# A gated recurrence followed by a maxout layer: folded weights, another opening order, and chunks turned block by block

## The chip, the core and the metric

The kernel runs on one core of a Trainium2 chip. The metric is the device time of one execution in microseconds (us), the median of several runs. Names used below: PE is TensorE (matrix products and transposes), PEld its weight loads, DVE is VectorE, ACT is ScalarE, POOL is GpSimd, SP is SyncE, whose queue issues most of the transfers.

## The reference

Two stages, one after the other. The first is a gated recurrence over the sequence, per batch and channel; the second takes the larger of two linear maps of its output and projects it back.

```python
# x, f_logit: (4, 6144, 256)   lower_bound: (256,)
sig = 1 / (1 + exp(-f_logit))
f = lower_bound + (1 - lower_bound) * sig
i = 1 - f
for t in range(S):
    h = f[:, t] * h + i[:, t] * x[:, t]
    y[:, t] = h
# y as 24576 rows of 256;  w1, w2: (256, 1024)   w_out: (1024, 256)
out = maximum(y @ w1, y @ w2) @ w_out
```

## The kernel before

The rows are cut into 48 blocks of 512. Two rewritings shape the kernel. With om = 1 - lower_bound and u = sigmoid(-f_logit), the input gate is i = om * u, so the factor om is taken out of the recurrence and folded into the weights. And maximum(h1, h2) = h1 + relu(h2 - h1), so the hidden layer is one product with om * (w2 - w1), followed by a relu; what belongs to h1 is a linear map w1 @ w_out, worked out once (w13). The products with the hidden layer (H), the relus (R) and the projections (P, L) are the bulk of the work.

The first four blocks (NP = 4) are loaded in fp32 and transposed on TensorE. All later blocks come in chunks of two (CB = 2): GpSimd issues a cast of the chunk to bf16 in DRAM, and the SP queue issues a transposing transfer from there into SBUF.

```python
def cast(c):                      # chunk c: 2 blocks of f_logit, then of x, into DRAM in bf16
    for name, src in (("fs", f_logit), ("xs", x)):
        nc.gpsimd.dma_start(out=spare[c % NS, name][:], in_=src[b, k * TB : (k + CB) * TB, :], ...)

def turn_dma(c):                  # one transposing transfer for f, one for x; ttpool has 3 buffers of each
    for s, name in enumerate(("fs", "xs")):
        t = ttpool.tile([P, KC, CB * TB], BF16, name=("fT", "xT")[s])
        turned[c, s] = t
        nc.sync.dma_start_transpose(out=t[:], in_=spare[c % NS, name][:])

def cast_behind(c):               # a copy of one column of fT: the next casts wait for its landing
    if c + 1 < NCH:
        last = CB * TB - 1
        nc.gpsimd.tensor_copy(out=held[:], in_=turned[c, 0][:, KC - 1, last : last + 1])
        cast(c + 1)
```

The weights are loaded in quarters of 256 columns (w11 is quarter 1 of w1, wo0 the first quarter of w_out's rows) and prepared on the chip:

```python
def diff(k, h, eng):              # D: wdf = w2 - w1, fp32, 128 x 256
    eng.tensor_tensor(out=wdf[:, h, cols], in0=w2n[:, h, cols], in1=w1n[:, h, cols], op=ALU.subtract)

def scale(k, h, on_dve):          # SC: wd = om * wdf, bf16
    o, i, m = wd[:, h, cols], wdf[:, h, cols], om[:, h : h + 1]
    if on_dve:
        nc.vector.tensor_scalar_mul(out=o, in0=i, scalar1=m)
    else:
        nc.scalar.activation(out=o, in_=i, func=AF.Copy, scale=m)
```

The order of the opening is given by two lists. Every engine works through its own instructions in the order of the list. A letter after the point names the engine (a ScalarE, v VectorE, p GpSimd).

```python
LOADS = """
f0a x0a f0b x0b w11 w21 w13 w23 w12 w22 wo1 w10 f1a w20 wo3 x1a f1b wo2 x1b wo0
f2b f2a x2a x2b f3 x3
"""
PLAN = """
G0a keeps_T TU0a keeps RW1.p F0a0.a V0a F0a1.v warm2 TV0a S0a0 G0b warm5 TU0b
...
"""
```

The items: G the sigmoid, V the product of u and x, TU and TV their transposes on TensorE, F the forget factor, S the scan (the recurrence itself), RW and RO the rounding of w1 and w_out to bf16, TW and KW the transposes of w1 and their copy out of PSUM, W the products for w13 and KL their copy, H hidden products (a and b are the halves of a block), R relus, P and L projections, O the copy of an output, warm products on zeros that keep TensorE busy, CA the start of the first chunk. W130 is W for quarter 0: it needs wo0.

Five PSUM buffers (ps_d) serve the hidden products and all transposes, three (ps_o) the outputs. After the opening comes a regular loop: for each block and each of 8 column groups, one hidden product with its relu and one part of the projection of the block before, with gate, drive, forget and scan of a later block placed at fixed points.

Of the kernel before, what the change touches and what calls it, by code (L numbers as in the profile page):

```python
# [9 lines left out]
BF16 = mybir.dt.bfloat16  # L10
ALU = mybir.AluOpType
# [5 lines left out]
def kernel(  # L17
# [36 lines left out]
    scratch = ctx.enter_context(  # L54
        tc.tile_pool(name="scratch", bufs=1, space=bass.MemoryType.DRAM)
    )
    ttpool = ctx.enter_context(tc.tile_pool(name="turned", bufs=3))
    midpool = ctx.enter_context(tc.tile_pool(name="mid", bufs=2))
    ypool = ctx.enter_context(tc.tile_pool(name="ypool", bufs=4))
    rpool = ctx.enter_context(tc.tile_pool(name="rpool", bufs=3 * FC))  # L60
# [113 lines left out]
            )  # L174

    def turn_dma(c):
        for s, name in enumerate(("fs", "xs")):
            t = ttpool.tile([P, KC, CB * TB], BF16, name=("fT", "xT")[s])
            turned[c, s] = t
            nc.sync.dma_start_transpose(out=t[:], in_=spare[c % NS, name][:])  # L180

    def cast_behind(c):

        if c + 1 < NCH:
            last = CB * TB - 1
            nc.gpsimd.tensor_copy(out=held[:], in_=turned[c, 0][:, KC - 1, last : last + 1])  # L186
            cast(c + 1)

    def part(j, s):
        c, o = divmod(j - NP, CB)  # L190
        return turned[c, s][:, :, o * TB : (o + 1) * TB]

    def gate(j):
        ffs[j] = midpool.tile([P, KC, TB], BF16, name="ff")
        ys[j] = ypool.tile([P, KC, TB], BF16, name="y")
        us[j] = midpool.tile([P, KC, TB], BF16, name="u")
        nc.scalar.activation(out=us[j][:], in_=part(j, 0), func=AF.Sigmoid, scale=-1.0)  # L197

    def drive(j):
        vs[j] = midpool.tile([P, KC, TB], BF16, name="v")  # L200
        nc.vector.tensor_tensor(out=vs[j][:], in0=us[j][:], in1=part(j, 1), op=ALU.mult)  # L201

    def forget_half(j, h, on_act=False):
        forget(ffs[j][:, h, :], us[j][:, h, :], h, on_act)
# [107 lines left out]
    def copy_out(j, g, on_act=False):  # L312
# [3 lines left out]
        else:  # L316
            nc.vector.tensor_copy(out=osbs[j, g][:], in_=pos[j, g, 0][:])  # L317

    def send_out(j, g):
        r0 = j * TB + 2 * g * P  # L320
        nc.sync.dma_start(
            out=out[r0 : r0 + 2 * P, :].rearrange("(p r) d -> p r d", r=2),
            in_=osbs[j, g][:],
        )

    def store(j, g):
        copy_out(j, g)
# [47 lines left out]
        )  # L375
        nc.vector.tensor_scalar_add(out=nom[:], in0=pt, scalar1=-1.0)

    def diff(k, h, eng):
        cols = slice(k * QF, (k + 1) * QF)
        eng.tensor_tensor(  # L380
            out=wdf[:, h, cols], in0=w2n[:, h, cols], in1=w1n[:, h, cols], op=ALU.subtract
        )

    def scale(k, h, on_dve):
        cols = slice(k * QF, (k + 1) * QF)
        o, i, m = wd[:, h, cols], wdf[:, h, cols], om[:, h : h + 1]
        if on_dve:
            nc.vector.tensor_scalar_mul(out=o, in0=i, scalar1=m)  # L388
        else:
            nc.scalar.activation(out=o, in_=i, func=AF.Copy, scale=m)  # L390

    def turn_w1(k):
        pts[k] = ps_d.tile([P, 2, D], BF16, name="dT")
# [49 lines left out]


    LOADS = """
    f0a x0a f0b x0b w11 w21 w13 w23 w12 w22 wo1 w10 f1a w20 wo3 x1a f1b wo2 x1b wo0
    f2b f2a x2a x2b f3 x3
    """
    PLAN = """
    G0a keeps_T TU0a keeps RW1.p F0a0.a V0a F0a1.v warm2 TV0a S0a0 G0b warm5 TU0b  # L450
    F0b0.a S0a1 D10.p RW3.p V0b warm5 TW1 D11.v F0b1.a SC11.a SC10.a TV0b D30.p S0b0
    S0b1 warm6 H02a H03a RW2.p D31.v SC31.v D21.v KW1.a TW3 H02b H03b SC30.a D20.p
    RW0.p RO1.v R02.a TW2 KW3.v SC21.a H06a H06b H07b R03.a H07a W131 SC20.v R06.v
    P020 H04a TW0 P031 H04b D01.p KW2.v P021 G1a KW0.v RO3.v D00.p R07.a R04.a V1a
    P030 TU1a H05a SC01.a H05b SC00.a G1b R05.a F1a1.v P060 F1a0.v P070 P071 P061
    W133 TV1a H00b RO2.p S1a1 V1b H01b TU1b H00a H01a F1b0.a W132 P050 P041 TV1b
    S1a0 P051 R01.a P040 R00.a RO0.a CA H10a H12a F1b1.v H11a G2b H16a P001 S1b0
    W130 G2a P000 S1b1 P010 H10b H16b KL1.v R10.v H11b KL0.a H12b P011 R12.a L00
    R11.a TU2a H14b V2b TU2b V2a H14a H17a R16.a H17b O00.a R14.a G3b L01 R17.a TV2a
    L11 F2a1.v L10 F2b1.v F2a0.v P160 F2b0.v TV2b P100 P120 TU3b P121 S2a0 H13b G3a  # L460
    F3b0.a O01.a S2b0 P140 S2a1 S2b1 H15b P101 H13a P161 P171 R13.a H15a F3b1.v TU3a
    R15.a H24 R24.a H22 V3a H26 F3a1.v F3a0.v R22.a V3b P111 TV3a P170 P141 H20 TV3b
    H23 R26.a P110 H21 S3a1 S3a0 S3b1 P130 P150 S3b0 R20.a H25 R23.a H27 R27.v R21.a
    P151 P131 O10.a R25.a O11.v
    """

    engines = {"a": nc.scalar, "v": nc.vector, "p": nc.gpsimd}
# [18 lines left out]
    def issue(item):  # L486
        name, _, e = item.partition(".")
        eng, on_dve, on_act = engines.get(e), e == "v", e == "a"
        kind = name.rstrip("0123456789ab")
        arg = ["ab".index(c) if c in "ab" else int(c) for c in name[len(kind) :]]  # L490
        if kind == "warm":
            keep_warm(arg[0])
        elif name == "keeps_T":
            turn_bound()
        elif name == "keeps":
            keeps()
        elif kind in ("G", "V") and len(arg) == 2:
            (gate_nat if kind == "G" else drive_nat)(arg[0], 2 * arg[1], 2 * arg[1] + 2)
        elif kind in ("TU", "TV"):
            turn_pe(arg[0], "UV".index(kind[1]), arg[1])  # L500
        elif kind == "F" and len(arg) == 3:
            j, x, h = arg
            tok = slice(x * HB, (x + 1) * HB)
            forget(ffs[j][:, h, tok], uT[j, x][:, h, :], h, on_act)
        elif kind == "S" and len(arg) == 3:
            j, x, h = arg
            scan(j, h, x * HB, (x + 1) * HB, vT[j, x][:, h, :])
        elif kind == "RW":
            round_w1(arg[0], eng)
        elif kind == "RO":  # L510
            round_wout(arg[0], eng)
        elif kind == "D":
            diff(arg[0], arg[1], eng)
        elif kind == "SC":
            scale(arg[0], arg[1], on_dve)
        elif kind == "TW":
            turn_w1(arg[0])
        elif kind == "KW":
            keep_w1(arg[0], eng)
        elif kind == "W":  # L520
            linear_weights(int(name[3]))
        elif kind == "KL":
            keep_linear(arg[0], on_dve)
        elif kind == "H":
            (hidden_half if len(arg) == 3 else hidden_whole)(*arg)
        elif kind == "R":
            relu(arg[0], arg[1], on_dve)
        elif kind == "P":
            pair_steps(arg[0], arg[2], [arg[1]])
        elif kind == "L":  # L530
            pair_steps(arg[0], arg[1], [FC, FC + 1])
        elif kind == "O":
            copy_out(arg[0], arg[1], on_act)
            outs.append(arg)
            send_pending()
        elif kind == "CA":
            nc.gpsimd.tensor_copy(out=held[:], in_=ins[2][1][:, 1, D - 1 : D])
            cast(0)
            turn_dma(0)
            cast_behind(0)  # L540
            send_pending()
        else:
            raise ValueError(item)
# [7 lines left out]
    with tc.manual_schedule():  # L551
        for j in range(NP):
            alloc_in(j)
        nc.scalar.dma_start(out=lbr[:], in_=lower_bound.rearrange("(h p) -> h p", p=P))
        for name in LOADS.split():
            load_item(name)
        nc.vector.memset(warm[:], 0.0)  # L557
        make_identity(nc, ident[:])
        nc.vector.tensor_copy(out=ident_b[:], in_=ident[:])
        keep_warm(7)  # L560
        for item in PLAN.split():
            issue(item)
        assert not outs

        for j in range(3, NBLK + 1):
            for fc in range(FC):
                if j < NBLK:
                    hidden(j, fc)
                project(j - 1, fc)
                if fc == 0 and j > 3:  # L570
                    store(j - 2, 1)
                if fc == 4 and j < NBLK:
                    store(j - 1, 0)
                if j == NBLK and fc in (3, 5, 7):
                    if fc == 3:
                        store(j - 1, 0)
                    else:
                        store_row(j - 1, 1, (fc - 5) // 2)
                if (j, fc) in gate_of:
                    b = gate_of[j, fc]  # L580
                    gate(b)
                    drive(b)
                    for h in range(KC):
                        forget_half(b, h, b == NP)
                        scan_half(b, h)
                if (j, fc) in turn_of:
                    turn_dma(turn_of[j, fc])
                    cast_behind(turn_of[j, fc])
# [30 lines left out]
```

## Time and profile before

| | |
|---|---|
| time, median of 3 runs | 397.82 us (397.27 to 398.25) |
| span of the profiled execution | 395.7 us |
| granted TensorE clock | 1.0 |
| PE busy | 390.5 us |
| ACT busy | 274.4 us |
| DVE busy | 251.3 us |
| POOL busy | 36.7 us |
| bytes moved by DMA | 79.12 MB |

Busy time is summed over the whole span. The products are pipelined and their ends are modelled, so a fully busy PE says only that it had no gap. A group line gives the source line of the kernel, the engine, the operation, what is written and read, and the count; in the timeline the first two columns are the start and the duration in us, and a bracket at the end gives the idle time of the engine just before and what ended it.

### The profile page before, as it was taken

The page shows a single profiled execution, that of the slowest core. Times are in us where ns is not written, and L with a number is a line of the kernel's source. Part 1 is how long each engine was busy: PE and PEld are TensorE (multiplying, and loading weights), DVE is VectorE, ACT ScalarE, POOL GpSimd, SP SyncE. Part 2 cuts the span into 40 slices and gives each one's busy share as a digit, 9 for nine tenths or more (in the row PEclk, how much of TensorE's full clock was granted, in tenths as well). Part 3 has the DMA queues.
Part 4 walks back from the last instruction along what each step waited for, and adds up shares of the span by engine and source line. Part 5 has one row for each costly group of instructions (what it writes and reads, how often), then busy time and mean ns, then how long its engine had stood idle before and what let it go on. Part 6 is the DMA issues. An engine that isn't in the chain of part 4 may idle for free.

```text
span 395.7 us, 7192 instructions
## 1 busy us (share of the span) xinstructions
PE 390.5 (99%) x2842; PEld 275.2 (70%) x2842; DVE 251.3 (63%) x365; ACT 274.4 (69%) x453; POOL 36.7 (9%) x82
## 2 busy tenths in 40 slices
PE   8999999999999999999999999999999999999996
PEld 4796777776666777776667777767677777676775
DVE  4886865756755775576567656755775576567622
ACT  3787876677667666766676677667766766676661
POOL 2511011001201101101101011011011010000000
PEclk9999999999999999999999999999999999999999
DMA  7999999999999999999889899999998999991122
GB/s 227 352 258 206 217 223 195 239 199 208 259 199 200 212 202 221 236 209 216 206 195 210 162 227 183 235 209 195 200 207 208 188 194 225 193 188 55 53 81 107
DMA packets 125078, 79.12 MB, mean 200 GB/s; under 512 B 94194, under 2 KB 101620, under 8 KB 125044
## 3 DMA queue, kind: packets, MB, share of 16 engines
q1 hardware_dynamic: 113072, 55.59, 57.5%
q0 software_dynamic: 11968, 23.07, 35.5%
q8 instruction: 22, 0.36, 0.4%
q14 instruction: 12, 0.10, 0.1%
q10 hardware_dynamic: 4, 0.00, 0.0%
HBM read 53.48 MB, written 48.23 MB: 257 GB/s over the span
## 4 chain that ended last, share of the span: by engine, by line
PE 96%; DMA 1%; DVE 1%; SPq 1%; issue 0%; DVEq 0%
PE psO L268 53%; PE dT L245 40%; PE dT L225 1%; DMA w2n<-in_moe_w_dram 1%; PE dT L126 1%; DVE wdf L380 0%; SPq L100 0%; PE psO L413 0%; DVE y L149 0%; SPq L344 0%; DVE row L332 0%; DVE w1T L355 0%; DVE wob L355 0%; DVE wd L388 0%; PE dT L396 0%
## 5 line engine op out<-in xcount | busy, mean ns | idle before, releaser
L240 ACT ACTIVATE rt<-dT 128x512 bf16<-128x512 f32 x381 | 222.6, 596 | 104.1 <-PE dT L245 102.3
L268 PE MATMUL psO<-wob,rt 128*128 128x256 bf16 x1536 | 230.4, 273 | 0.0
L245 PE MATMUL dT<-y,wd 128*128 128x512 bf16 x736 | 218.4, 379 | 0.0
L268 PEld LDWEIGHTS <-rt 128*128 128x128 bf16 x1536 | 150.1, 98 | 94.9
L149 DVE TENSOR_TENSOR_SCAN y<-ff,y,v 128x512 bf16<-128x512 bf16 x82 | 105.2, 1283 | 2.9
L317 DVE COPY osb<-psO 128x512 f32<-128x512 f32 x92 | 62.1, 679 | 66.9 <-PE psO L268 66.9
L245 PEld LDWEIGHTS <-wd 128*128 128x128 bf16 x736 | 71.9, 98 | 8.9
L268 PE MATMUL psO<-w,y 128*128 128x256 bf16 x384 | 72.4, 273 | 0.0
L201 DVE TENSOR_TENSOR v<-u,xT 128x1024 bf16<-128x1024 bf16 x44 | 30.4, 692 | 61.2 <-ACT u L197 52.2
L197 ACT ACTIVATE u<-fT 128x1024 bf16<-128x1024 bf16 x44 | 46.1, 1048 | 1.2 <-DMA fT<-fs 1.1
L268 PEld LDWEIGHTS <-y 128*128 128x128 bf16 x384 | 37.5, 98 | 4.3
L186 POOL CAST held<-fT 128x1 f32<-128x1 bf16 x21 | 4.7, 226 | 279.4 <-DMA fT<-fs 279.4
L138 DVE TENSOR_SCALAR ff<-u,nom 128x512 bf16<-128x512 bf16 x86 | 29.1, 339 | 0.0
L170 POOL DMA_DIRECT2D fs<-in_f_logit_dram x22 | 12.3, 558 | 5.2 <-issue 5.0
L170 POOL DMA_DIRECT2D xs<-in_x_dram x22 | 12.1, 549 | 0.3 <-issue 0.3
L149 DVE TENSOR_TENSOR_SCAN y<-nff,y,dT 128x256 bf16<-128x256 bf16 x14 | 9.8, 735 | 2.2 <-PE dT L126 2.1
L225 PE MATMUL dT<-y,wd 128*128 128x256 bf16 x64 | 9.8, 273 | 1.0 <-DVE w1T L355 0.8
L433 PE MATMUL psO<-warm 128*128 128x512 bf16 x25 | 8.5, 484 | 1.2 <-DVE warm L557 1.2
L149 DVE TENSOR_TENSOR_SCAN y<-ff,v 128x512 bf16<-128x512 bf16 x6 | 7.4, 1225 | 0.2
L225 PEld LDWEIGHTS <-wd 128*128 128x128 bf16 x64 | 5.9, 98 | 2.2 <-issue 1.0
L108 ACT ACTIVATE un<-fn 128x512 bf16<-128x512 f32 x8 | 5.1, 637 | 1.9 <-DMA fn<-in_f_logit_dram 1.5
L433 PEld LDWEIGHTS <-warm 128*128 128x128 bf16 x25 | 2.7, 120 | 4.0 <-issue 1.8
(42 smaller groups left out, 58.2 us busy)
## 6 DMA issues: line engine op xcount, KB each, us to landing
out_dram<-osb SPq DMA_DIRECT2D x95, 256.0 KB, 3.2
fs<-in_f_logit_dram POOLq DMA_DIRECT2D x22, 512.0 KB, 6.6
xs<-in_x_dram POOLq DMA_DIRECT2D x22, 512.0 KB, 9.5
fn<-in_f_logit_dram SPq DMA_DIRECT2D x6, 256.0 KB, 6.0
xn<-in_x_dram SPq DMA_DIRECT2D x6, 256.0 KB, 5.3
w1n<-in_moe_w_dram SPq DMA_DIRECT2D x4, 256.0 KB, 6.0
w2n<-in_moe_w_dram SPq DMA_DIRECT2D x4, 256.0 KB, 6.0
won<-in_moe_w_out_dram SPq DMA_DIRECT2D x4, 256.0 KB, 6.2
```

Of the source, the lines that this page charges most:

```text
L108: nc.scalar.activation(out=us[j][:, q0:q1, :], in_=ins[j][0][:, q0:q1, :], func=AF.Sigmoid, scale=-1.0)
L138: nc.vector.tensor_scalar(out=o, in0=i, scalar1=nom[:, h : h + 1], scalar2=1.0, op0=ALU.mult, op1=ALU.add)
L149: nc.vector.tensor_tensor_scan(out=ys[j][:, h, t0:t1], data0=ffs[j][:, h, t0:t1], data1=v, initial=initial, op0=ALU.mult, op1=ALU.add,)
L170: nc.gpsimd.dma_start(out=spare[c % NS, name][:], in_=src[b, k * TB : (k + CB) * TB, :], max_dma_last_dim=4096,)
L197: nc.scalar.activation(out=us[j][:], in_=part(j, 0), func=AF.Sigmoid, scale=-1.0)
L201: nc.vector.tensor_tensor(out=vs[j][:], in0=us[j][:], in1=part(j, 1), op=ALU.mult)
L225: nc.tensor.matmul(dts[j, fc][:, tok], lhsT=wd[:, kc, unit(fc)], rhs=ys[j][:, kc, tok], start=(first and kc == 0), stop=(not first and kc ...
L240: nc.scalar.activation(out=rt[:], in_=dts[j, fc][:], func=AF.Relu)
L245: nc.tensor.matmul(dts[j, fc][:], lhsT=wd[:, kc, unit(fc)], rhs=ys[j][:, kc, :], start=(kc == 0), stop=(kc == KC - 1),)
L268: nc.tensor.matmul(ps, lhsT=lhsT, rhs=rhs, start=start, stop=stop, skip_group_check=True)
L317: nc.vector.tensor_copy(out=osbs[j, g][:], in_=pos[j, g, 0][:])
L433: nc.tensor.matmul(idle[:].rearrange("p r d -> p (r d)"), lhsT=warm[:, 0:P], rhs=warm[:], start=True, stop=True,)
```

## The change

It has five parts.

1. The weights are folded as om * w2 - om * w1. The first product (item A) needs w1 alone and may run on any engine; the second (item B) is one fused multiply and subtract on VectorE. It is meant to shorten what follows the landing of w2.
2. The order of the loads and of the opening's list is new; three quarters of w1 are loaded ahead of w2. The item CA stands at the end of the list, and the first casts wait for the landing of f's second half of block 2 (before: of x's first half).
3. A chunk is turned block by block: four transposes (f and x of the first block, then of the second) into six smaller buffers of each kind.
4. The copy that holds the next casts back reads the x of the chunk's first block instead of the f of the whole chunk. It is meant to bound what the casts collide with.
5. In the loop the forget factors are worked out ahead of the drive product, and the stores of blocks 45 and 46 are split in two.

```diff
-    ttpool = ctx.enter_context(tc.tile_pool(name="turned", bufs=3))
+    ttpool = ctx.enter_context(tc.tile_pool(name="turned", bufs=6))
...
     def turn_dma(c):
-        for s, name in enumerate(("fs", "xs")):
-            t = ttpool.tile([P, KC, CB * TB], BF16, name=("fT", "xT")[s])
-            turned[c, s] = t
-            nc.sync.dma_start_transpose(out=t[:], in_=spare[c % NS, name][:])
+        b0, n = NP + c * CB, CB
+        for o in range(n):
+            for s, name in enumerate(("fs", "xs")):
+                t = ttpool.tile([P, KC, TB], BF16, name=("fT", "xT")[s])
+                turned[b0 + o, s] = t
+                nc.sync.dma_start_transpose(
+                    out=t[:], in_=spare[c % NS, name][o * TB : (o + 1) * TB, :]
+                )

     def cast_behind(c):
         if c + 1 < NCH:
-            last = CB * TB - 1
-            nc.gpsimd.tensor_copy(out=held[:], in_=turned[c, 0][:, KC - 1, last : last + 1])
+            b0, n = NP + c * CB, CB
+            nc.gpsimd.tensor_copy(out=held[:], in_=turned[b0, n - 1][:, KC - 1, TB - 1 : TB])
             cast(c + 1)
...
     def send_out(j, g):
+        if NBLK - 4 < j < NBLK - 1:
+            for r in range(2):
+                nc.sync.dma_start(out=rows_out(j, g)[:, r, :], in_=osbs[j, g][:, r, :])
+        else:
+            nc.sync.dma_start(out=rows_out(j, g), in_=osbs[j, g][:])
...
-    def diff(k, h, eng):
+    def fold_w1(k, h, eng):
         cols = slice(k * QF, (k + 1) * QF)
-        eng.tensor_tensor(
-            out=wdf[:, h, cols], in0=w2n[:, h, cols], in1=w1n[:, h, cols], op=ALU.subtract
-        )
-
-    def scale(k, h, on_dve):
+        o, i, m = wdf[:, h, cols], w1n[:, h, cols], om[:, h : h + 1]
+        if eng is nc.scalar:
+            nc.scalar.activation(out=o, in_=i, func=AF.Copy, scale=m)
+        else:
+            eng.tensor_scalar_mul(out=o, in0=i, scalar1=m)
+
+    def fold_diff(k, h):
         cols = slice(k * QF, (k + 1) * QF)
...
+        nc.vector.scalar_tensor_tensor(
+            out=wd[:, h, cols],
+            in0=w2n[:, h, cols],
+            scalar=om[:, h : h + 1],
+            in1=wdf[:, h, cols],
+            op0=ALU.mult,
+            op1=ALU.subtract,
+        )
...
     LOADS = """
-    f0a x0a f0b x0b w11 w21 w13 w23 w12 w22 wo1 w10 f1a w20 wo3 x1a f1b wo2 x1b wo0
-    f2b f2a x2a x2b f3 x3
+    f0a x0a f0b x0b w12 w11 w13 w21 wo1 w23 w22 wo3 f1a w10 w20 x1a f1b wo2 x1b wo0
+    f2a x2a f2b x2b f3 x3
     """
     PLAN = """
-    G0a keeps_T TU0a keeps RW1.p F0a0.a V0a F0a1.v warm2 TV0a S0a0 G0b warm5 TU0b
-    F0b0.a S0a1 D10.p RW3.p V0b warm5 TW1 D11.v F0b1.a SC11.a SC10.a TV0b D30.p S0b0
-    S0b1 warm6 H02a H03a RW2.p D31.v SC31.v D21.v KW1.a TW3 H02b H03b SC30.a D20.p
-    RW0.p RO1.v R02.a TW2 KW3.v SC21.a H06a H06b H07b R03.a H07a W131 SC20.v R06.v
-    P020 H04a TW0 P031 H04b D01.p KW2.v P021 G1a KW0.v RO3.v D00.p R07.a R04.a V1a
-    P030 TU1a H05a SC01.a H05b SC00.a G1b R05.a F1a1.v P060 F1a0.v P070 P071 P061
-    W133 TV1a H00b RO2.p S1a1 V1b H01b TU1b H00a H01a F1b0.a W132 P050 P041 TV1b
-    S1a0 P051 R01.a P040 R00.a RO0.a CA H10a H12a F1b1.v H11a G2b H16a P001 S1b0
-    W130 G2a P000 S1b1 P010 H10b H16b KL1.v R10.v H11b KL0.a H12b P011 R12.a L00
...
+    G0a V0a keeps_T TU0a warm1 TV0a keeps A20.p F0a1.a S0a1 G0b RW1.p F0a0.a warm7
+    TU0b V0b F0b0.a S0a0 A11.p warm2 TV0b F0b1.a RW2.a A31.p A10.a S0b0 S0b1 B10 B11
+    warm4 TW2 TW1 RW3.a KW1.a warm2 TW3 RO1.a A21.v A30.p warm3 H03a H02a H03b B31
+    B30 KW2.a KW3.v B21 B20 H02b RO3.p W131 H06a R02.a H06b A00.p R06.v R03.a RW0.v
+    H07a P020 P021 H07b G1a W133 H05a H05b R07.a P061 A01.p H04a R05.a H04b B00 TW0
+    TU1a RO2.p B01 V1a P070 P030 H00a R04.a F1a1.v H01b H01a KW0.a TV1a P031 P060
+    F1a0.v G1b H00b TU1b S1a1 P071 R01.a V1b S1a0 P051 P050 W132 R00.a P040 F1b0.a
+    TV1b P041 H10a H14a F1b1.a H16a H13a S1b0 RO0.a G2a S1b1 W130 V2a P001 KL0.a
+    P010 H13b H10b P000 R13.v H16b TU2a F2a1.v H14b KL1.a L00 R10.a G2b R14.v P011
+    R16.a V2b L01 TU2b TV2a P161 F2a0.a O00.a H17b F2b0.v L11 H12a G3a H17a H15b
...
     """
...
         elif kind == "CA":
-            nc.gpsimd.tensor_copy(out=held[:], in_=ins[2][1][:, 1, D - 1 : D])
+            nc.gpsimd.tensor_copy(out=held[:], in_=ins[2][0][:, 3, D - 1 : D])
...
                     gate(b)
+                    for h in range(KC):
+                        forget_half(b, h, b == NP)
                     drive(b)
                     for h in range(KC):
-                        forget_half(b, h, b == NP)
                         scan_half(b, h)
```

More of the change, by code (lines that the diff above doesn't have):

```diff
@@ L176, in turn_dma @@
     def turn_dma(c):
-        for s, name in enumerate(("fs", "xs")):
-            t = ttpool.tile([P, KC, CB * TB], BF16, name=("fT", "xT")[s])
-            turned[c, s] = t
-            nc.sync.dma_start_transpose(out=t[:], in_=spare[c % NS, name][:])
+        b0, n = NP + c * CB, CB
[6 more added lines that the diff above has]
+                )
     def cast_behind(c):
         if c + 1 < NCH:
-            last = CB * TB - 1
-            nc.gpsimd.tensor_copy(out=held[:], in_=turned[c, 0][:, KC - 1, last : last + 1])
+            b0, n = NP + c * CB, CB
+            nc.gpsimd.tensor_copy(out=held[:], in_=turned[b0, n - 1][:, KC - 1, TB - 1 : TB])
             cast(c + 1)
-    def part(j, s):
-        c, o = divmod(j - NP, CB)
-        return turned[c, s][:, :, o * TB : (o + 1) * TB]
     def gate(j):
@@ L196, in gate @@
         us[j] = midpool.tile([P, KC, TB], BF16, name="u")
-        nc.scalar.activation(out=us[j][:], in_=part(j, 0), func=AF.Sigmoid, scale=-1.0)
+        nc.scalar.activation(out=us[j][:], in_=turned[j, 0][:], func=AF.Sigmoid, scale=-1.0)
     def drive(j):
         vs[j] = midpool.tile([P, KC, TB], BF16, name="v")
-        nc.vector.tensor_tensor(out=vs[j][:], in0=us[j][:], in1=part(j, 1), op=ALU.mult)
+        nc.vector.tensor_tensor(out=vs[j][:], in0=us[j][:], in1=turned[j, 1][:], op=ALU.mult)
     def forget_half(j, h, on_act=False):
@@ L317, in copy_out, with rows_out @@
             nc.vector.tensor_copy(out=osbs[j, g][:], in_=pos[j, g, 0][:])
+    def rows_out(j, g):
+        r0 = j * TB + 2 * g * P
+        return out[r0 : r0 + 2 * P, :].rearrange("(p r) d -> p r d", r=2)
     def send_out(j, g):
[L320 to L323, printed above, removed]
-        )
+        if NBLK - 4 < j < NBLK - 1:
[3 more added lines that the diff above has]
+            nc.sync.dma_start(out=rows_out(j, g), in_=osbs[j, g][:])
     def store(j, g):
@@ L376, in keeps @@
         nc.vector.tensor_scalar_add(out=nom[:], in0=pt, scalar1=-1.0)
-    def diff(k, h, eng):
+    def fold_w1(k, h, eng):
         cols = slice(k * QF, (k + 1) * QF)
-        eng.tensor_tensor(
-            out=wdf[:, h, cols], in0=w2n[:, h, cols], in1=w1n[:, h, cols], op=ALU.subtract
-        )
-    def scale(k, h, on_dve):
[L385 to L390, printed above, removed]
+        o, i, m = wdf[:, h, cols], w1n[:, h, cols], om[:, h : h + 1]
[4 more added lines that the diff above has]
+    def fold_diff(k, h):
+        cols = slice(k * QF, (k + 1) * QF)
+        nc.vector.scalar_tensor_tensor(
[5 more added lines that the diff above has]
+            op1=ALU.subtract,
+        )
     def turn_w1(k):
@@ L453 @@
-    RW0.p RO1.v R02.a TW2 KW3.v SC21.a H06a H06b H07b R03.a H07a W131 SC20.v R06.v
-    P020 H04a TW0 P031 H04b D01.p KW2.v P021 G1a KW0.v RO3.v D00.p R07.a R04.a V1a
-    P030 TU1a H05a SC01.a H05b SC00.a G1b R05.a F1a1.v P060 F1a0.v P070 P071 P061
-    W133 TV1a H00b RO2.p S1a1 V1b H01b TU1b H00a H01a F1b0.a W132 P050 P041 TV1b
-    S1a0 P051 R01.a P040 R00.a RO0.a CA H10a H12a F1b1.v H11a G2b H16a P001 S1b0
-    W130 G2a P000 S1b1 P010 H10b H16b KL1.v R10.v H11b KL0.a H12b P011 R12.a L00
-    R11.a TU2a H14b V2b TU2b V2a H14a H17a R16.a H17b O00.a R14.a G3b L01 R17.a TV2a
@@ L460 @@
[L460 to L464, printed above, removed]
+    G0a V0a keeps_T TU0a warm1 TV0a keeps A20.p F0a1.a S0a1 G0b RW1.p F0a0.a warm7
+    TU0b V0b F0b0.a S0a0 A11.p warm2 TV0b F0b1.a RW2.a A31.p A10.a S0b0 S0b1 B10 B11
@@ new lines @@
+    P010 H13b H10b P000 R13.v H16b TU2a F2a1.v H14b KL1.a L00 R10.a G2b R14.v P011
+    R16.a V2b L01 TU2b TV2a P161 F2a0.a O00.a H17b F2b0.v L11 H12a G3a H17a H15b
+    R17.a F2b1.v S2a1 H15a S2a0 P101 H12b TV2b S2b1 R15.a R12.a P140 P100 S2b0 TU3a
+    P170 G3b F3a0.v H11a O01.a F3a1.v L10 H11b P141 H20 R11.a P131 H27 R27.a H22 V3a
+    H25 R20.v V3b P121 TV3a R22.a S3a1 TU3b P171 R25.a S3a0 P160 H21 TV3b P110
+    F3b0.a P150 H24 P120 F3b1.a H23 P151 R21.a R24.a S3b0 P111 S3b1 H26 P130 R26.v
@@ L465 @@
+    R23.a O11.a O10.v CA
     """
@@ L511, in issue @@
             round_wout(arg[0], eng)
[L512 to L515, printed above, removed]
+        elif kind == "A":
+            fold_w1(arg[0], arg[1], eng)
+        elif kind == "B":
+            fold_diff(*arg)
         elif kind == "TW":
```

## The prediction

> **What bounds the kernel now.** I read the page first: busy times, slices, and the chain that ended last.
>
> ```profile
> PE 390.5 (99%) x2842; PEld 275.2 (70%) x2842; DVE 251.3 (63%) x365; ACT 274.4 (69%) x453; POOL 36.7 (9%) x82
> ...
> PE   8999999999999999999999999999999999999996
> ...
> DMA  7999999999999999999889899999998999991122
> ...
> PE 96%; DMA 1%; DVE 1%; SPq 1%; issue 0%; DVEq 0%
> ```
>
> TensorE carries 96% of the chain and is full from the second slice to the last; the other compute engines are below 70%. The DMA engines look full too, so they are the first rival. A busy TensorE may still be doing nothing useful, because the opening runs products on zeros. So next I cut the span into stages (columns: stretch, its length, then busy time and instructions of PE, PEld, DVE, ACT, POOL, the granted clock, the DMA share and GB/s).
>
> ```profile
> 13.70:392.40 378.70, 378.70 (x2776) 269.33 (x2775) 242.55 (x347) 267.50 (x441) 31.25 (x70) 1.00 0.94 198
> 0.00:13.70 13.70, 11.55 (x66) 5.92 (x67) 8.29 (x18) 6.92 (x13) 5.45 (x13) 1.00 0.82 263
> ```
>
> From 13.70 us TensorE never stops. No product is removed by the change, so it can win only the part of the first 13.70 us that isn't useful work, or lose by a new hole later. The timeline of TensorE shows that opening.
>
> ```profile
> 9.31 1.46 PE L433 MATMUL psO<-warm 128*128 128x512 bf16 x6
> 10.88 0.61 PE L225 MATMUL dT<-y,wd 128*128 128x256 bf16 x4
> 11.33 0.39 PE L396 MATMUL dT<-ident_b,w1b 128*128 128x128 bf16 x4
> 11.55 0.60 PE L225 MATMUL dT<-y,wd 128*128 128x256 bf16 x4
> 12.02 0.40 PE L396 MATMUL dT<-ident_b,w1b 128*128 128x128 bf16 x4
> 12.26 0.60 PE L225 MATMUL dT<-y,wd 128*128 128x256 bf16 x4
> 13.70 0.60 PE L225 MATMUL dT<-y,wd 128*128 128x256 bf16 x4 [0.84 <-DVE w1T L355]
> ```
>
> The first real products start at 10.88; the next hole ends at 13.70, released by VectorE's copy of w1T, which frees a PSUM buffer. VectorE's own timeline says why that copy was late.
>
> ```profile
> 8.90 0.99 DVE L380 TENSOR_TENSOR wdf<-w2n,w1n 128x256 f32<-128x256 f32 x1 [0.64 <-DMA w2n<-in_moe_w_dram]
> ...
> 11.10 0.40 DVE L380 TENSOR_TENSOR wdf<-w2n,w1n 128x256 f32<-128x256 f32 x1
> ...
> 12.03 0.94 DVE L380 TENSOR_TENSOR wdf<-w2n,w1n 128x256 f32<-128x256 f32 x1
> 12.90 0.41 DVE L355 CAST wob<-won 128x512 bf16<-128x512 f32 x1
> 13.24 0.41 DVE L355 COPY w1T<-dT 128x512 bf16<-128x512 bf16 x1
> ```
>
> The same subtraction takes 0.40 or 0.94 to 0.99 us. The long ones began while GpSimd ran one of its own (8.88 to 9.60 and 11.93 to 12.70).
>
> **What the Trainium skill says.** "SBUF — State Buffer", section "Who interferes with whom": a VectorE instruction with two SBUF inputs competes with a GpSimd instruction that reads SBUF; the later one waits for the whole of the other. The three subtractions agree: 0.40 against 0.94 and 0.99. The new fused operation also has two SBUF inputs, so it can be held in the same way. "VectorE: DVE Perf Modes", section on the fixed extra latency of SBUF sources: an fp32 two-tensor operation takes (N+151)/0.96 ns, that is 424 ns at N=256; the trace has 396. I take 0.40 us for the fused operation too: an estimate, since no row here holds one. "DMA: Bandwidth & Descriptors", "Specifications", gives some 358 GB/s from HBM to a core; here the loads move 351 GB/s between 9 and 24 us. So the loads arrive at a fixed pace, and their order is what can be chosen.
>
> **The change part by part.** I use one unit: a group of two 256-wide products, or of four 128-wide transposes. Between 13.70 and the product W130 (which needs the last quarter to arrive of w_out, wo0) at 22.02 stand 38 such units by the plan: 8.32/38 = 0.219 us each. Before 13.70, 13 units were done (4 input transposes, 3 of w1, 6 of hidden products), so 13.70 - 13 x 0.219 = 10.85 us of TensorE were lost.
>
> *Landings.* By issue and time to landing, the loads in places 5 to 20 land at 8.1, 8.8, 9.5, 10.3 (between its neighbours), 11.0, 11.8, 12.6, 13.3, 14.1, 14.8, 15.6, 16.3, 17.1, 17.8, 18.6 and 20.8. The new order puts w1's quarters 2, 1, 3 in places 5 to 7, w2's quarter 1 in 8, wo1 in 9, w2's 3 and 2 in 10 and 11, wo3 in 12.
>
> *Fold.* Before: subtract (0.40 to 0.99), then a scaling after it (ScalarE 0.51, VectorE 0.55 to 0.58), both after w2. Now om*w1 needs w1 alone and only one operation of 0.40 follows w2. First hidden products: w2's quarter 1 lands at 10.3 instead of 8.8 (1.5 later), the two fused operations run to about 11.1, or 11.6 if GpSimd's A30 and A31 hold them. They start at 11.1 to 11.6 instead of 10.88, so the first product is later by 0.2 to 0.7. Quarter 3: 11.8, two operations, 12.7; quarter 2: after the w1T copy (0.41), 13.8. TensorE from 11.4: four units to 12.3, W131 to 12.7, then H06a straight away, and six units later quarter 2 is there. So it is full from about 12.8, with 13 units done: 12.8 - 13 x 0.219 = 9.95 us lost, against 10.85. **First sum: -0.9 us.**
>
> *What takes it back.* ScalarE rounds the last w_out quarter as soon as it lands.
>
> ```profile
> 20.88 0.62 ACT L355 CAST wob<-won 128x512 bf16<-128x512 f32 x1 [0.20 <-DMA won<-in_moe_w_out_dram]
> ...
> 22.02 0.60 PE L413 MATMUL psO<-wob,w1T 128*128 128x256 bf16 x4
> ```
>
> wo0 is in place 20 in both orders. In the new plan 50 units precede W130 (51 before). Undisturbed it would be reached at 9.95 + 50 x 0.219 = 20.9; but the rounded quarter can't be there before 20.83 + 0.05 + 0.62 + 0.06, about 21.56. TensorE would wait 0.66. Then 21.56 - 50 x 0.219 = 10.61 is lost, against 10.85. **Second sum: -0.24 us.** If wo0 keeps the 0.75 spacing of its predecessors (it came 2.2 after the one in front), nothing is taken back.
>
> *Transposes block by block.* Two chunk transposes become four half ones; bytes and issue time (2.69 and 2.27 us median) stay about the same. The next casts now wait for the first block's f and x, instead of for the whole f. Those waits hardly reach anyone now:
>
> ```profile
> ACT u L197 <- DMA fT<-fs: 1.1, 1, 1.1
> ...
> DVE v L201 <- DMA xT<-xs: 1.5, 1, 1.5
> ```
>
> In steady state a chunk takes TensorE 2 x 7.82 = 15.6 us, and the early gates fall 13.0 to 15.9 us apart. Waiting for x costs up to 3 us of casting once. An estimate of the new chain: casts 10, the transpose of x about 4, gate 0.5: 14.5, still under 15.6. I put 0 here.
>
> *Forget before drive, split stores.* VectorE waits for u either way (52.2 us, off the path): 0. The split stores are of blocks 45 and 46, after the bulk of the DMA: 0 to 0.1 at the tail, whose row copy and last store aren't changed.
>
> **Rivals.** (1) *The opening gains in full*, because wo0 lands at about 19.4: -0.9, 396.9. For it: the 2.2 us step looks like an accident of one transfer. Against it: total bytes and queue are the same. (2) *The DMA becomes the bound*, four small transposes and a later gate costing more than a chunk's slack: each us over 15.6 comes back up to 20 times, 400 to 415. For it: the DMA row of nines. Against it: 14.5 against 15.6, and the slack of several us visible in one short wait out of 44. (3) *New holes in blocks 1 to 3*: V2a stands ahead of R13, R14 and the block 2 work on VectorE and waits for x2a (about 22.3), with five PSUM buffers in turn: +0.3 to +1.0, so 397.9 to 398.6. For it: that one queue stop. Against it: ScalarE serves R10 and R16 beside it.
>
> **Range and chances.** The second sum gives 397.6, the first 396.9; the third rival pulls up. I take 397.4, and 396.4 to 398.5, which also covers the spread of the time before (397.27 to 398.25). Two per cent are 8 us: the opening hasn't that much to give, since more than 5 us of its loss is waiting for the first bytes. Faster by over 2%: 0.01. Slower: 0.02, all of it rival 2.
>
> **What would show it.** Right: first hidden products at 11.1 to 11.6, TensorE full from about 12.8, then one wait on ScalarE's wob before W130 near 21.5; fused operations of 0.4 us, or about 0.9 beside GpSimd; 15.6 us per chunk after. Rival 1: W130 before 21.2 without a wait. Rival 2: TensorE waiting for scans, VectorE for xT, after 60 us. Rival 3: TensorE gaps between 22 and 35 us. I am wrong if the full stage starts after 13.5, or if more than 0.5 us of TensorE gaps stand after 23.

## The result and the profile after

The changed kernel is slower than the one before: ratio 1.010, 95% interval 1.0057 to 1.0142, some 4 us. Its four executions took 400.84, 402.52, 407.19 and 409.70 us, where those of the kernel before stay within 397.27 to 398.25. The ratios here leave out executions over 1.5% longer than the same kernel's fastest, of this kernel the last two, so its loss may be understated. The profiled execution is the fastest; its span is 399.1 us, 3.4 more than before. The page, by the same lines as were read before:

```profile
PE 390.4 (98%) x2796; PEld 274.7 (69%) x2843; DVE 247.4 (62%) x363; ACT 274.3 (69%) x456; POOL 40.7 (10%) x81
...
DMA  7999998999999999999999999999998999989523
...
PE 84%; DMA 10%; ACT 3%; issue 1%; SPq 1%; POOL 1%; DVE 0%; ACTq 0%
```

The busy times hardly moved, and the row of TensorE is the same. The row of the DMA engines ends in 9523 instead of 1122: the transfers no longer finish ahead of the products. The chain moved most: transfers now hold 10% of it instead of 1%, 7% of it the transposes of f. A row of tenths is too coarse for small holes, so the stages have to be asked for (columns: stretch, length, busy time and count of PE, PEld, DVE, ACT, POOL, clock, DMA share, GB/s):

```profile
300.00:350.00 50.00, 48.54 (x337) 33.06 (x342) 29.61 (x42) 32.45 (x54) 5.00 (x9) 1.00 1.00 193
350.00:380.00 30.00, 29.48 (x207) 20.35 (x210) 19.09 (x28) 21.04 (x35) 1.67 (x3) 1.00 0.80 194
```

In the kernel before, TensorE was full here (its line from 13.70 to 392.40 in the prediction). Some matmul records are missing, so a second clock is wanted: VectorE's copy of each finished output. Up to 298 us it starts at nearly the same time in both kernels (79.42 and 79.55, 298.38 and 298.51); at the end it is at 390.49 and 393.83. So the opening cost 0.13 us, and the other 3.2 us came after 298 us, in steps. The chain that ended last names them (start, duration, what):

```profile
296.18 5.28 DMA fT<-fs
301.57 1.06 ACT u L197
302.62 1.47 ACT rt L240 x3
...
312.77 5.37 DMA fT<-fs
318.25 1.06 ACT u L197
...
329.73 5.08 DMA fT<-fs
```

Each time a transpose of f comes too late: ScalarE, which works in order, stands before its sigmoid, the relus behind it are late, and TensorE waits for those. The totals of the waits for these transfers (total us, times, longest) were 1.1 and 1.5 before:

```profile
ACT u L197 <- DMA fT<-fs: 15.0, 10, 2.8
DVE v L201 <- DMA xT<-xs: 10.6, 10, 3.3
```

The steps are 16.6 and 17.0 us apart, one per chunk, and a chunk costs TensorE 15.64 (two blocks of 7.82). They come late because the kernel starts with blocks in hand: up to 182 us no sigmoid waits for its f. The first that does waits 0.84 us, and the wait has grown to 2.77 at 318.25; the first small waits don't reach TensorE.

```profile
190.90 1.06 ACT L197 ACTIVATE u<-fT 128x1024 bf16<-128x1024 bf16 x1 [0.84 <-DMA fT<-fs]
```

So the transfers use up the lead and then set the pace. GpSimd's copy that lets the next casts go marks each turn:

```profile
304.11 0.64 POOL L190 CAST held<-xT 128x1 f32<-128x1 bf16 x1 [15.18 <-DMA xT<-xs]
304.68 0.55 POOL L170 DMA_DIRECT2D fs<-in_f_logit_dram  x1
...
321.28 0.64 POOL L190 CAST held<-xT 128x1 f32<-128x1 bf16 x1 [15.51 <-DMA xT<-xs]
321.86 0.55 POOL L170 DMA_DIRECT2D fs<-in_f_logit_dram  x1
```

The SP queue shows what lies between (start and duration of each issue):

```profile
304.50 1.99 SPq L328 DMA_DIRECT2D out_dram<-osb  x4
312.77 1.23 SPq L182 DMA_TRANSPOSE fT<-fs  x1
317.46 1.23 SPq L182 DMA_TRANSPOSE xT<-xs  x1
318.78 1.25 SPq L182 DMA_TRANSPOSE fT<-fs  x1
320.08 1.29 SPq L182 DMA_TRANSPOSE xT<-xs  x1
```

One turn: the cast of f from 304.68 to 312.77, when its first transpose can be issued, 8.1; then the wait for the cast of x, 4.7; its transpose lands 3.8 later; 0.6 to the next cast. Sum 17.2. It is the longest turn of the run; their mean is 15.91. The second f, whose data has been there since 312.77, is issued at 318.78, behind the x. The stores of the outputs stand in the same queue and come four at once just as the next casts begin (304.50). The queue's waits say the same of the whole run, first of the kernel before, then of the changed one:

```profile
SPq L180 <- DMA fs<-in_f_logit_dram: 24.7, 7, 10.5
...
SPq L180 <- DMA xs<-in_x_dram: 0.2, 1, 0.2
```

```profile
SPq L182 <- DMA fs<-in_f_logit_dram: 112.4, 21, 9.6
SPq L182 <- DMA xs<-in_x_dram: 49.6, 22, 3.4
```

Before, the casts had mostly landed when the queue came to a transpose; now it waits for them in 21 and 22 of 22 chunks. A wait for f is no loss by itself, as e7 will show: it has 22 of them and none for x.

The opening went as follows on TensorE:

```profile
11.50 1.04 PE L225 MATMUL dT<-y,wd 128*128 128x256 bf16 x8
...
12.91 0.83 PE L225 MATMUL dT<-y,wd 128*128 128x256 bf16 x6
...
17.59 0.72 PE L225 MATMUL dT<-y,wd 128*128 128x256 bf16 x5 [0.41 <-DVE wd L394]
...
21.93 0.60 PE L424 MATMUL psO<-wob,w1T 128*128 128x256 bf16 x4
```

It is full from 12.91, but has a new hole before 17.59: the fused operations on VectorE wait there for GpSimd, which takes 2.05 us for two products om * w1:

```profile
14.96 2.05 POOL L389 TENSOR_SCALAR wdf<-w1n,om 128x256 f32<-128x256 f32 x2 [0.91 <-DMA w1n<-in_moe_w_dram]
```

### The profile page after: what moved, and what is told of

It reads as the page before. It is cut to its first block, busy times and chain, and to the rows that moved or that the text cites. A ratio compares the mean times of both kernels' runs of the same rounds, so it can differ in the third digit from the quotient of the medians.

```text
span 399.1 us, 7198 instructions
## 1 busy us (share of the span) xinstructions
PE 390.4 (98%) x2796; PEld 274.7 (69%) x2843; DVE 247.4 (62%) x363; ACT 274.3 (69%) x456; POOL 40.7 (10%) x81
## 4 chain that ended last, share of the span: by engine, by line
PE 84%; DMA 10%; ACT 3%; issue 1%; SPq 1%; POOL 1%; DVE 0%; ACTq 0%
PE psO L268 47%; PE dT L245 35%; DMA fT<-fs 7%; DMA w1n<-in_moe_w_dram 3%; ACT rt L240 2%; ACT u L197 1%; PE dT L225 1%; PE dT L126 1%; POOL wdf L389 1%; SPq L100 0%; PE psO L424 0%; DVE wd L394 0%; SPq L348 0%; DVE row L336 0%; ACTq L197 0%
## 5 line engine op out<-in xcount | busy, mean ns | idle before, releaser
L240 ACT ACTIVATE rt<-dT 128x512 bf16<-128x512 f32 x379 | 219.0, 596 | 95.9 <-PE dT L245 91.9
L245 PE MATMUL dT<-y,wd 128*128 128x512 bf16 x690 | 208.7, 379 | 2.1
L149 DVE TENSOR_TENSOR_SCAN y<-ff,y,v 128x512 bf16<-128x512 bf16 x82 | 100.9, 1271 | 1.5
L138 DVE TENSOR_SCALAR ff<-u,nom 128x512 bf16<-128x512 bf16 x86 | 26.5, 351 | 67.8 <-ACT u L197 67.8
L190 POOL CAST held<-xT 128x1 f32<-128x1 bf16 x21 | 8.5, 403 | 296.2 <-DMA xT<-xs 296.2
L170 POOL DMA_DIRECT2D xs<-in_x_dram x22 | 12.1, 551 | 0.0
L113 DVE TENSOR_TENSOR vn<-un,xn 128x512 bf16<-128x512 bf16 x8 | 5.4, 681 | 2.9 <-DMA xn<-in_x_dram 2.8
L389 POOL TENSOR_SCALAR wdf<-w1n,om 128x256 f32<-128x256 f32 x6 | 5.8, 975 | 7.6 <-DMA w1n<-in_moe_w_dram 7.6
## 6 DMA issues: line engine op xcount, KB each, us to landing
xs<-in_x_dram POOLq DMA_DIRECT2D x22, 512.0 KB, 10.8
```

The costliest lines, as they stand in the source:

```text
L138: nc.vector.tensor_scalar(out=o, in0=i, scalar1=nom[:, h : h + 1], scalar2=1.0, op0=ALU.mult, op1=ALU.add)
L149: nc.vector.tensor_tensor_scan(out=ys[j][:, h, t0:t1], data0=ffs[j][:, h, t0:t1], data1=v, initial=initial, op0=ALU.mult, op1=ALU.add,)
L240: nc.scalar.activation(out=rt[:], in_=dts[j, fc][:], func=AF.Relu)
L245: nc.tensor.matmul(dts[j, fc][:], lhsT=wd[:, kc, unit(fc)], rhs=ys[j][:, kc, :], start=(kc == 0), stop=(kc == KC - 1),)
L389: eng.tensor_scalar_mul(out=o, in0=i, scalar1=m)
```

## Experiments

Four theories were on the table. A: the gate (GpSimd's copy), since the next casts wait for x too. B: four smaller transposes cost the DMA engines more. C: the opening or the split stores. D, formed after the first four runs: the order f, x, f, x. Every run is compared with executions of the kernel before on the same chip.

### e1: the gate alone, on the first f

```diff
-  in_=turned[b0, n - 1][:, KC - 1, TB - 1 : TB]
+  in_=turned[b0, 0][:, KC - 1, TB - 1 : TB]
```

> The changed kernel with one edit: the copy that holds the next casts back reads the f of the chunk's first block instead of its x; the four block transposes stay. Theory A (the gate: the next casts wait for xs, then for its transpose, so one chunk's chain is longer than the 15.6 us that TensorE needs for it): the wait of some 4 us leaves the chain, casts start 13 to 15 us apart where TensorE isn't the pace, and the time is 397.4 to 398.2, that of before within 0.1%. Theory B (the four smaller transposes cost the DMA engines more than two large ones, and they are the bound): still above 400. Theory C (the opening or the split stores): still above 400.

Measured: 406.73 us, ratio 1.0191 (1.0133 to 1.0248). The earlier gate doesn't help, so A alone falls. The gate on x came out lower (1.010), but the two intervals overlap.

### e2: the kernel before with the gate on x

```diff
-  in_=turned[c, 0][:, KC - 1, last : last + 1]
+  in_=turned[c, 1][:, KC - 1, last : last + 1]
```

> The kernel before with one edit: the copy that holds the next casts back reads the x of the whole chunk (xT) instead of its f; two large transposes, old opening. Theory A: the chain is xs (10 to 12 us) plus the large transpose of x (4.5) plus the issue (0.6), 15.1 to 17.1 us against 15.6, so 399 to 406 us. Theory B and C: 397.3 to 398.2, as before.

Measured: 397.76 us, ratio 0.9998 (0.999 to 1.0007). Waiting for x costs nothing here, where no transpose is left to run beside the next casts.

### e3: the kernel before with block-by-block turning

The functions of the change in the kernel before, with the gate on the first f; opening, forget order and stores as before.

```diff
-  ttpool = ctx.enter_context(tc.tile_pool(name="turned", bufs=3))
+  ttpool = ctx.enter_context(tc.tile_pool(name="turned", bufs=6))
   # turn_dma as in the change: four transposes, f, x, f, x
-  in_=turned[c, 0][:, KC - 1, last : last + 1]
+  in_=turned[b0, 0][:, KC - 1, TB - 1 : TB]
```

> The kernel before with the chunks turned block by block (four smaller transposes, six buffers of each kind) and the next casts held back by the f of the first block; old opening, old order of forget and drive, stores not split. Theory A: 397.3 to 398.2. Theory B: above 400.

Measured: 415.55 us, ratio 1.0336 (1.0308 to 1.0365). Block-by-block turning with its gate makes the loss without the rest of the change, and a larger one. Why it is larger than in e1, which has the same turning and gate, stays open.

### e4: the changed kernel with the turning of before

Two large transposes, the gate on the whole f; fold, opening, forget order and split stores as changed.

```diff
-  ttpool = ctx.enter_context(tc.tile_pool(name="turned", bufs=6))
+  ttpool = ctx.enter_context(tc.tile_pool(name="turned", bufs=3))
   # turn_dma and cast_behind as in the kernel before
```

> The changed kernel with the turning of before: two large transposes per chunk, the next casts held back by the f of the whole chunk; new fold, new opening, forget ahead of drive and split stores stay. Theory A and B: 397.7 to 398.2, the 0.1 to 0.3 us that the trace shows the opening to lose. Theory C: above 400.

Measured: 398.02 us, ratio 1.0008 (1.0002 to 1.0015). C falls as the main cause; opening, forget order and split stores together cost 0.3 us. After these four, B stood, but so did something that goes with it: the order.

### e5: order f, f, x, x, gate on the second f

```diff
-  for o in range(n):
-      for s, name in enumerate(("fs", "xs")):
+  for s, name in enumerate(("fs", "xs")):
+      for o in range(n):
...
-  in_=turned[b0, n - 1][:, KC - 1, TB - 1 : TB]
+  in_=turned[b0 + n - 1, 0][:, KC - 1, TB - 1 : TB]
```

> The changed kernel with its four smaller transposes in the order f, f, x, x instead of f, x, f, x, and the next casts held back by the second f (as in the kernel before, where the whole f holds them back). Theory B (smaller transposes cost more each): above 400. Theory D (the order: the second f has to stand behind the first x, which waits for the cast of x; so three of the four transposes, instead of two, come after that cast and run into the next one): 397.6 to 398.6, as with the large transposes, with casts 15.0 to 15.4 us apart.

Measured: 397.85 us, ratio 1.0004 (0.9996 to 1.0013). B falls: as many small transposes, and the loss is gone.

### e7: the order alone

The first edit of e5 only; the gate stays on the x of the first block.

```diff
-  for o in range(n):
-      for s, name in enumerate(("fs", "xs")):
+  for s, name in enumerate(("fs", "xs")):
+      for o in range(n):
```

> The changed kernel with the order f, f, x, x alone changed; the next casts stay held back by the x of the first block. Theory B: above 400. Theory D: 397.6 to 398.8; only one transpose is then left to run beside the next casts.

Measured: 397.78 us, ratio 1.0003 (0.9994 to 1.0011). Two loops exchanged undo the whole loss. On its SP queue both f are now issued ahead of the x, the two x come together, and the stores are spread over 7.73 us instead of 1.99:

```profile
275.97 7.73 SPq L328 DMA_DIRECT2D out_dram<-osb  x4
284.37 4.67 SPq L182 DMA_TRANSPOSE fT<-fs  x2
289.14 2.59 SPq L182 DMA_TRANSPOSE xT<-xs  x2
...
300.72 4.88 SPq L182 DMA_TRANSPOSE fT<-fs  x2
305.70 2.59 SPq L182 DMA_TRANSPOSE xT<-xs  x2
```

Its queue still waits for the cast of f, and for the cast of x no longer:

```profile
SPq L182 <- DMA fs<-in_f_logit_dram: 56.9, 22, 10.0
```

### e6: large transposes, x ahead of f

```diff
-  for s, name in enumerate(("fs", "xs")):
+  for s, name in ((1, "xs"), (0, "fs")):
...
-  in_=turned[c, 0][:, KC - 1, last : last + 1]
+  in_=turned[c, 1][:, KC - 1, last : last + 1]
```

> The kernel before, two large transposes per chunk, but x ahead of f, and the next casts held back by x, the first of them to land. No transpose can start before the cast of x has landed; the transpose of f runs into the next casts. Theory B: 397.3 to 398.2, as before, since nothing is made smaller. Theory D: above 400, since all the transposing now comes after the casts; the cycle is then casts 10 to 12, x 4.5, issue 0.6 and more where f collides, 15.5 to 17 us.

Measured: 409.75 us, ratio 1.0295 (1.026 to 1.033). A loss, and a larger one, made in the kernel before without making any transpose smaller. From e2, which also has its gate on x, it differs by the order alone. D stands from both sides.

### e12: casts one chunk further ahead

The order and gate of the change stay.

```diff
-  NS = 2
+  NS = 3
...
-            cast(c + 1)
+            if c == 0:
+                cast(1)
+            if c + 2 < NCH:
+                cast(c + 2)
```

> The changed kernel with the order f, x, f, x and the gate on x kept, but with the casts one chunk further ahead (three buffers in DRAM instead of two, the gate of chunk c lets the casts of chunk c+2 start, the first gate those of chunks 1 and 2). The transposes then find both casts landed and never stand behind one that waits. If the order costs only because the transposes wait inside one chain of casts and transposes (latency): 397.6 to 398.6. If the interleaved transposes and the casts beside them are too much for the DMA engines whatever the waits (throughput): above 400.

Measured: 402.09 us, ratio 1.011 (1.0073 to 1.0148). By the total this is the throughput forecast, and the total misleads. One of the four executions was traced (401.55 us). It has one loss early, where two chunks of casts were let go at once and one transpose of f took 11 us:

```profile
44.24 11.08 DMA fT<-fs
```

After that nothing is lost any more: VectorE's output copies are 4.04 us behind the kernel before at 79.42 and 4.04 behind at the last one (394.53 against 390.49), and TensorE has no gap (columns as above):

```profile
80.00:390.00 310.00, 310.00 (x2223) 217.26 (x2221) 190.16 (x270) 218.19 (x356) 22.90 (x52) 1.00 0.95 192
```

With casts ahead, the queue waits for them three times in all:

```profile
SPq L182 <- DMA fs<-in_f_logit_dram: 9.7, 1, 9.7
SPq L182 <- DMA xs<-in_x_dram: 3.6, 2, 2.3
```

So in this trace the DMA engines carry the order f, x, f, x at TensorE's pace. It is the chain of waits that can't, not their throughput.

### e8: one product of the fold off GpSimd

On top of e4; A00 is the product om * w1 of quarter 0, first half.

```diff
-  ... H06a R02.a H06b A00.p R06.v R03.a RW0.v
+  ... H06a R02.a H06b R06.v R03.a RW0.v A00.v
```

> The kernel of the run with the turning of before (large transposes) and the new opening, with one product of the fold, om times w1 for quarter 0 and the first half, moved from GpSimd to VectorE right behind the rounding of that quarter. In the changed kernel GpSimd takes 2.05 us for the two products and TensorE waits for them up to 17.59. Fold theory: the first hidden product of quarter 0 starts near 17.0 and the time falls by 0.3 to 0.6, to 397.2 to 397.7. If instead the landing of the last quarter of w_out is what counts by then, the time stays at 397.8 to 398.1.

Measured: 397.55 us, ratio 0.9996 (0.9988 to 1.0004). The hole is gone: the first product of quarter 0 is in the group at 16.56, and W130 starts at 21.01 instead of 21.93. The interval overlaps that of e4; what the edit is worth is settled by e11.

```profile
16.56 0.84 PE L225 MATMUL dT<-y,wd 128*128 128x256 bf16 x6
```

### e9 and e10: stores whole, and another product on ScalarE

e9 is e8 with every output stored whole:

```diff
-  if NBLK - 4 < j < NBLK - 1:
-      for r in range(2):
-          nc.sync.dma_start(out=rows_out(j, g)[:, r, :], in_=osbs[j, g][:, r, :])
-  else:
-      nc.sync.dma_start(out=rows_out(j, g), in_=osbs[j, g][:])
+  nc.sync.dma_start(out=rows_out(j, g), in_=osbs[j, g][:])
```

e10 is e9 with

```diff
-  ... TW3 RO1.a A21.v A30.p warm3
+  ... TW3 A30.a RO1.a A21.v warm3
```

> The kernel of the opening run (large transposes, new opening, one product of the fold moved to VectorE) with the stores of blocks 45 and 46 left whole. The last products ended 0.8 us earlier there than in the kernel before, the time fell by 0.3 at most. If the split stores cost at the tail: 0.2 to 0.3 less than that run, 397.2. If they don't: 397.4 to 397.6, the same.

> As the run with whole stores, and the product of the fold for quarter 3, first half, moved from GpSimd to ScalarE, so that GpSimd no longer reads SBUF while VectorE runs the fused operations of quarters 1 and 3. If the hole of 0.25 us before 12.83 and the length of those operations come from GpSimd: TensorE is full from about 12.6 and the time falls by another 0.2 to 0.4, 396.9 to 397.2. Else no change.

Measured: e9 397.20 us, ratio 0.9985 (0.9979 to 0.9992); e10 397.04 us, ratio 0.9987 (0.998 to 0.9993). Both beat the kernel before by some 0.6 us. The intervals of e8 and e9 overlap, so nothing is shown of the split stores. e10 isn't better than e9. In its trace, of its slowest execution (398.17), ScalarE waits 0.98 us for a landing before it rounds quarter 3 of w1, and the first products start at 12.28.

### e11: the change, mended

The changed kernel with the edits of e7 and e8; small transposes, gate on x and split stores stay.

```diff
-  for o in range(n):
-      for s, name in enumerate(("fs", "xs")):
+  for s, name in enumerate(("fs", "xs")):
+      for o in range(n):
...
-  ... H06a R02.a H06b A00.p R06.v R03.a RW0.v
+  ... H06a R02.a H06b R06.v R03.a RW0.v A00.v
```

> The changed kernel whole, with two mends: the order f, f, x, x of the four transposes, and the product of the fold for quarter 0, first half, on VectorE. Theory D and fold theory together: the DMA keeps ahead and the opening gains: 397.2 to 397.6, below the kernel before by 0.1 to 0.5. If smaller transposes or the gate on x still cost something: 397.8 or more.

Measured: 397.17 us, ratio 0.9983 (0.9976 to 0.9989). Faster than both, by 0.6 us than the kernel before. From e7 (0.9994 to 1.0011) it differs by the product of the fold alone, and the intervals don't meet: the product on GpSimd had cost 0.002, some 0.8 us. Its chain is TensorE's again:

```profile
PE 94%; DMA 5%; SPq 0%; ACT 0%; DVE 0%; issue 0%
```

## Why the prediction was wrong

**The failed step** is "Transposes block by block", where I put 0. It stood on a chain of "casts 10, the transpose of x about 4, gate 0.5: 14.5, still under 15.6". The form was right and the transpose and gate terms too (3.8 and 0.6), but in the late turn shown the casts took 12.8, and 17.2 is over 15.6. Over the whole run the median cast of x takes 10.8 us instead of 9.5, and the spacing is 15.91. The landing times I had used are those of the kernel before, in whose order no f stands behind an x.

Rival 2 came true in its number (400 to 415), but not by its causes: four small transposes cost nothing by themselves (e5, e7), nor does the later gate (e2). That the order of the four would matter stood neither in the estimate nor in a rival. The sign named for being wrong, over 0.5 us of TensorE gaps after 23, came with the 3.2 us after 298.

What fits all runs is that two things count: whether the next casts wait for x, and how much transposing is still to be done when they start. For the second there are pairs that differ by the order alone, e2 with e6 and e7 with the changed kernel. The first is argued from the table: where the gate alone differs (before and e2, e5 and e7, e1 and the changed kernel), waiting for x made no kernel slower. (Waits and shares follow from the order. Casts: median from issue to landing, of f and of x. Spacing: mean distance of GpSimd's gates, from the second to the last.)

| kernel | casts wait for x | transposing left | casts f, x, us | spacing, us | ratio |
|---|---|---|---|---|---|
| before | no | 1/2 | 6.6, 9.5 | 15.06 | 1 |
| e4 | no | 1/2 | 6.8, 10.0 | 15.10 | 1.0008 |
| e2 | yes | 0 | 5.6, 9.2 | 15.31 | 0.9998 |
| e7 | yes | 1/4 | 5.9, 9.2 | 15.25 | 1.0003 |
| after | yes | 1/2 | 7.7, 10.8 | 15.91 | 1.010 |
| e6 | yes | 1/2 | 7.6, 10.0 | 16.11 | 1.0295 |
| e1 | no | 3/4 | 8.7, 11.5 | 16.01 | 1.0191 |
| e3 | no | 3/4 | 7.9, 11.3 | 16.34 | 1.0336 |

Every kernel with a spacing over 15.64 is slow, and none under it is. (e12, whose loss came in one early piece, is not in the table: 15.22.) The two columns part slow from not slow; the size of a loss they don't give, as after and e6 or e1 and e3 show. The order f, x, f, x leaves more behind because the second f stands in the queue behind an x whose cast hasn't landed. I had read that in the diff and counted only bytes and issue time.

The casts of f are slower in every kernel with the loss (7.6 to 8.7 us) than in the others (5.6 to 6.8). What slows them isn't separated. Beside the transposes the held-up stores run too: the median landing of a store is 3.2 us before, 2.9 in e7, 7.2 in the changed kernel, though only 3.7 in e6. No run moves the stores to settle it.

**Why the profile didn't warn me.** I took "one short wait out of 44" for "slack of several us". A wait total shows only what slack is used up; the slack per turn was in the gates' spacing, and I had that view. In the kernel before, the nine turns between these two gates take 14.4 us each, so the slack was some 1.2 us a turn; the late turns (288.70, 304.29, 319.96) are 15.6 and 15.7 apart, TensorE's own pace.

```profile
50.22 0.18 POOL L186 CAST held<-fT 128x1 f32<-128x1 bf16 x1 [14.37 <-DMA fT<-fs]
...
179.70 0.18 POOL L186 CAST held<-fT 128x1 f32<-128x1 bf16 x1 [12.31 <-DMA fT<-fs]
```

And the loss grows with the number of turns after the lead is gone, so a small excess looks like nothing for 298 us.

**The opening.** First hidden products at 11.1 to 11.6: right, 11.50. Full from about 12.8: right, 12.91. Fused operations 0.4, or 0.9 if held: the eight took 0.47 to 0.83, with a median of 0.48. The one at 16.15 took 0.69 beside a product on GpSimd that ran on to 17.01, so it wasn't held to the other's end as the prediction allowed. W130 near 21.5 after a wait on the last quarter of w_out: wrong twice. ScalarE rounded that quarter at 20.49 without a wait: it had landed at 19.38, 0.73 after the load in front, as rival 1 had it. The 2.2 us step was an accident of single traces: e2, with the loads of before, has 0.74, and e11, with the new ones, 2.28. Yet W130 came at 21.93, mostly for the hole before 17.59: the 37 units from 12.91 on would take 8.1 us by the prediction's 0.219, and took 9.0. The missing term is GpSimd's product, 0.91 to 1.15 us each, which I hadn't put in the sum at all. So the second sum's -0.24 is +0.13 in the trace and +0.3 by e4, which has the forget order and split stores too. With the product moved (e8) W130 is at 21.01, close to the undisturbed 20.9 of the first sum.

**Forget order and split stores.** 0 expected; e7 and e11 contain both and show no loss. Rival 3, new holes in blocks 1 to 3, didn't come: the lag is 0.13 from there on.

## What to carry to other kernels

In a queue that works in order, a transfer that waits for its source holds every ready one behind it, so transfers are ordered by when their sources land, not by who will use them first. Where the fetching is a chain that lets itself go again, compare the length of one turn, with the collisions it will then have, with the consumer's turn; the difference times the number of turns says how large the loss can be. Here 20 turns give 5.4, 7.4, 9.4 and 14.0 us for the changed kernel, e1, e6 and e3; their traced spans are 3.4, 9.3, 12.1 and 14.4 us longer, so it is a rough size. A profile whose busy times don't change can still have changed its bound: look at the spacing of one marker per turn.

## What the runs showed of the hardware

Splitting a transposing transfer of 512 KB in two costs nothing here that can be measured (e5, e7: 1.0004 and 1.0003), with both f ahead of both x. GpSimd's product of 128x256 fp32 by a scalar per partition took 0.91 to 1.15 us in the changed kernel, more than its cast of 128x512 at 0.60 to 0.66; VectorE took 0.40 and 0.47 (e8) and 0.56 (the changed kernel) for the same product.
